# A conversion piece moved between angle and sine, and another order of the first weight loads, in a fused attention, mixture-of-experts and feed-forward kernel

## The chip, the cores and the metric

The kernel runs on one core of a Trainium2 chip. The metric is device microseconds for one execution; lower is better. The engines are TensorE (PE, its weight loads apart as PEld), VectorE (DVE), ScalarE (ACT), GpSimd (POOL) and SyncE (SP), which issues most of the DMAs.

## The reference, cut to what matters

Three stages follow one another. The change is in the third, and its weights are the only thing of it that earlier stages touch.

```python
# attention with a sigmoid: x = concat over heads of sigmoid(q k^T / 8 - log 448) v   -> [1792, 768]
# mixture of experts, top 1 of 8 by the gate, two matmuls with a relu, scaled           -> [1792, 768]
def _moe2_ref(x, w_in, w_out):          # x [1792, 768], w_in [768, 2048], w_out [2048, 768]
    h = x @ w_in
    g = h * np.cos(h)
    return (g @ w_out).astype(np.float32)
```

The inputs of the feed-forward weights arrive as float64, 512 of them per partition in a piece, and have to be turned into pairs of float32 numbers (high and low part) before TensorE can use them.

## The kernel before

**Conversion.** `w_in` and `w_out` are cut into 48 pieces, listed in `conv_list`: six of `w_in`, six of `w_out`, and so on. `conv_step(False)` does the following for the next piece: it finishes the piece before it (`conv_end`), stores that piece's two halves to DRAM (`conv_store`: `wi_d` or `wo_d` from `chi` and `clo`, 256 KB each, on SP's queue), loads the raw data of the piece after it (`conv_load`: `craw`, 512 KB, two buffers, SP's queue), and runs the first half of its own piece. The first half (L154 to L158) is an absolute value and a copy on ACT, a maximum on POOL, and two operations on DVE. The second half (L160 to L163) is four operations on DVE. It runs at the next `conv_end`, which stands in `product`, behind the product and ahead of the split into high and low parts; `load_w` calls `conv_end` too, where the weight to be loaded needs that piece. Of the 48 pieces, 23 are begun in the attention stage and 17 in the expert stage, so eight (40 to 47) are left for the feed-forward.

**Feed-forward.** The tokens are handled in four blocks of 3 or 4 times 128 tokens, and the 2048 inner columns in 16 chunks of 128. A unit u is one block and one chunk. For each unit there is:

- `load_w(u)`: the weights `wi` (768 KB) and `wo` (768 KB) of the chunk, on SP's queue, into rings of six buffers; it also stores what pieces are finished. `er` is the first buffer of the ring for `wi`; it is loaded for unit 0 in the expert stage already
- `up(u)`: 18 matmuls (L1109 to L1111) into a PSUM tile `ph`, from one pair of banks that the transposes below share
- `take(u)`: ACT copies `ph` to `p` (L1118)
- `angle(u)`: five operations on DVE (L1123 to L1127), from `p` to `r`
- `cosine(u)`: an absolute value and a sine on ACT (L1132, L1133), on `r`
- `product(u)`: `r` times `p` on DVE (L1138), then the second half of a piece if one is open, then the split: `gh` on ACT (L1142), `gl` on DVE (L1143)
- `down(u)`: 24 matmuls (L1169, L1170) with `gh`, `gl` and `wo`

All engines work in program order. The loop is pipelined: iteration u does `load_w(u + 5)`, `product(u + 1)`, `up`, `take` and `angle` of u + 2, `cosine(u + 2)` and `down(u)`. In iterations 8 to 13 of a block, `turn_y` also transposes 128 columns of the next block's tokens between `up(u + 2)` and `down(u)` (four transposes on PE, L1094, a copy on ACT, L1096, a subtraction on DVE, L1098). In iterations 1 to 4 a gather of the next block's tokens is issued on POOL's queue. Before the loop, `turn_first` transposes the first block, and units 0 to 2 are begun.

Of the kernel before, what the change touches and what calls it, by code (L numbers as in the profile page):

```python
# [54 lines left out]
def tile_attn_moe_cos(ctx: ExitStack, tc: tile.TileContext, q, k, v, wg, wog, w1, w2, w_in, w_out, out):  # L55
# [66 lines left out]
    conv_list = []  # L122
# [7 lines left out]
    def conv_load(i):  # L130
        if i >= len(conv_list):
            return
        which, h, r = conv_list[i]
        raw = craw[i % 2]
        if which == "i":
            src = w_in[r * P : (r + 1) * P, h * CW : (h + 1) * CW].bitcast(U32)
            nc.sync.dma_start(raw.rearrange("p f t -> p (f t)"), src)
        else:
            src = wo_in[h][:, :, r * CO : (r + 1) * CO].bitcast(U32)
            nc.sync.dma_start(raw.rearrange("p (two f) t -> p two (f t)", two=2), src)  # L140

    def conv(i):
        if i >= len(conv_list):
            return
        which, h, r = conv_list[i]
        raw = craw[i % 2]
        low, high = raw[:, :, 0], raw[:, :, 1]

        ta = cta
        tb = conv_p.tile([P, CW], U32, tag="ctb", name="ctb")  # L150
        tu = conv_p.tile([P, CW], F32, tag="ctu", name="ctu")
        hi = conv_p.tile([P, CW], U32, tag="chi", name="chi", bufs=2)
        lo = conv_p.tile([P, CW], F32R, tag="clo", name="clo", bufs=2)
        nc.scalar.activation(ta.bitcast(F32), high.bitcast(F32), AF.Abs)  # L154
        nc.gpsimd.tensor_scalar(ta.bitcast(F32), ta.bitcast(F32), LEAST, None, op0=ALU.max)  # L155
        nc.scalar.activation(tu, low, AF.Copy, scale=2.0**-52)
        nc.vector.tensor_scalar(tb, high, 0x1FF, None, op0=ALU.bitwise_and)
        nc.vector.scalar_tensor_tensor(tu, tb, 2.0**-20, tu, op0=ALU.mult, op1=ALU.add)  # L158
        yield
        nc.vector.tensor_scalar(ta, ta, 3, 0x3FFFF000, op0=ALU.logical_shift_left, op1=ALU.bitwise_and)  # L160
        nc.vector.scalar_tensor_tensor(hi, high, 0xC0000000, ta, op0=ALU.bitwise_and, op1=ALU.bitwise_or)  # L161
        nc.vector.tensor_scalar(tb, hi, 0xFF800000, None, op0=ALU.bitwise_and)
        nc.vector.tensor_tensor(lo, tu, tb.bitcast(F32), op=ALU.mult)  # L163
        conv_out.append((which, h, r, (hi.bitcast(F32), lo.bitcast(F32))))

    def conv_store():
        while conv_out:
            which, h, r, parts_ = conv_out.pop()
            for t, f in enumerate(parts_):
                if which == "i":  # L170
                    c0 = h * CW // P
                    nc.sync.dma_start(
                        wi_d[c0 : c0 + CW // P, :, t, r, :].rearrange("c p f -> p c f"),
                        f.rearrange("p (c f) -> p c f", f=P),
                    )
                else:
                    nc.sync.dma_start(
                        wo_to[h, t][:, :, r * CO : (r + 1) * CO], f.rearrange("p (two f) -> p two f", two=2)
                    )

    conv_at = [0]

    def conv_step(whole=True):
        conv_end()
        conv_store()
        conv_load(conv_at[0] + 1)
        conv_rest.append(conv(conv_at[0]))
        next(conv_rest[0], None)
        conv_at[0] += 1
        if whole:  # L190
            conv_end()
# [3 lines left out]
    def conv_end():  # L195
        while conv_rest:
            next(conv_rest.pop(), None)
# [444 lines left out]
    def load_w(u, which="io"):  # L642
        c = u % NFF
        ready = max(i for i, (which, h, _) in enumerate(conv_list) if h == (c * P // CW if which == "i" else c // 2))
        while conv_at[0] <= ready:
            conv_step()
        if conv_at[0] - 1 <= ready:
            conv_end()
        conv_store()
        if "i" in which:  # L650
            wi = ring_i[u % NRING]
            nc.sync.dma_start(wi.bitcast(F32), wi_d[c].rearrange("p t k f -> p (t k f)"))
            wi = wi.rearrange("p (t k f) -> p t k f", t=2, k=KD)
            parts["i", u] = (wi[:, 0], wi[:, 1])
        if "o" in which:
            wo = ring_o[u % NRING]
            nc.sync.dma_start(wo.bitcast(F32), wo_d[c * P : (c + 1) * P].rearrange("p t e -> p (t e)"))
            parts["o", u] = (wo[:, :DM], wo[:, DM:])
# [386 lines left out]
    with ExitStack() as st:  # L1045
# [12 lines left out]
        def take_ids(bi):  # L1058
            t0, nt = blocks[bi]
            for i in range(nt):  # L1060
                nc.vector.tensor_copy(tids[:, t0 + i : t0 + i + 1], ygt[i][:, DM : DM + 1].bitcast(I32))

        def turn_first():
            t0, nt = blocks[0]
            yh = yp.tile([P, KD, 512], F32R, tag="yh", name="yh")
            yl = yp.tile([P, KD, 512], F32R, tag="yl", name="yl")
            yts[0] = (yh, yl)
            spare = [ps_o.tile([P, 512], F32, tag=f"o{i}", name="pt") for i in range(3)]
            spare = [t[:, : 3 * P].rearrange("p (k t) -> p k t", t=P) for t in spare]
            for k0 in range(0, KD, 3):  # L1070
                for i in range(nt):
                    cols = slice(i * P, (i + 1) * P)
                    pt = spare[(i + nt * (k0 // 3)) % len(spare)]
                    for kc in range(3):
                        nc.tensor.transpose(
                            pt[:, kc, :], ygt[i][:, (k0 + kc) * P : (k0 + kc + 1) * P], ident
                        )
                    yhv, ylv = yh[:, k0 : k0 + 3, cols], yl[:, k0 : k0 + 3, cols]
                    nc.scalar.activation(yhv, pt, AF.Copy)
                    nc.vector.tensor_tensor(ylv, pt, yhv.bitcast(F32), op=ALU.subtract)  # L1080
            take_ids(0)
# [34 lines left out]
        def take(u, ph):  # L1116
            p = gpool.tile([P, 512], F32, tag="p", name="p", bufs=2)[:, : ph.shape[1]]
            nc.scalar.activation(p, ph, AF.Copy)  # L1118
            return p
# [10 lines left out]
        def cosine(u):  # L1130
            p, r = rs[u]
            nc.scalar.activation(r, r, AF.Abs)  # L1132
            nc.scalar.activation(r, r, AF.Sin, bias=b_half, scale=-1.0)  # L1133
# [15 lines left out]
        def down(u):  # L1149
# [14 lines left out]
            for i in range(nt):  # L1164
# [13 lines left out]
                if c == NFF - 1 and (own or i % 2 == 1):  # L1178
                    for j in (i,) if own else (i - 1, i):
# [3 lines left out]
                        done.append((t0 + j, osb))  # L1183
                    if u == N - 1:
                        put()

        def put():
            if done:
                i, osb = done.pop(0)

                at = yp.tile([P, 1], I32, tag="at", name="at", bufs=4)
                nc.gpsimd.tensor_copy(at, tids[:, i : i + 1])
                rows = nc.gpsimd.indirect_dma_start(  # L1193
                    out=out[:, :],
                    out_offset=bass.IndirectOffsetOnAxis(ap=at, axis=0),
                    in_=osb,
                    in_offset=None,
                )
                if i > 0:
                    tc.declare_no_dep(rows.ins, group="rows", reason="rows apart")  # L1200
                tc.add_to_no_dep_group("rows", rows.ins)

        N = len(units)
        conv_load(conv_at[0])
        load_w(0, "o")
        load_w(1)
        load_w(2)
        turn_first()
        load_w(3)
        p0 = take(0, up(0))  # L1210

        nc.scalar.activation(scs[:, 0:1], b_half, AF.Sin)
# [7 lines left out]
        cosine(1)  # L1220
        for u in range(N):
            bi, c = units[u]
            if u > 1 and conv_at[0] < len(conv_list):
                conv_step(False)
            if u + 5 < N:
                load_w(u + 5)
            turn = ()
            if bi + 1 < len(blocks):
                if 1 <= c < 5:
                    gather_y(bi + 1, c - 1)  # L1230
                if 8 <= c < 8 + KD:
                    turn = turn_y(bi + 1, c - 8)
            if u + 1 < N:
                product(u + 1)
            if u + 2 < N:
                angle(u + 2, take(u + 2, up(u + 2)) if u > 0 else p2)
            for _ in turn:
                pass
            if c < NFF - 1 and u + 2 < N:
                cosine(u + 2)  # L1240
            down(u)
            if c > 1:
                put()
            if c == NFF - 1 and u + 2 < N:
                cosine(u + 2)
# [28 lines left out]
```

## Time and profile before

| | |
|---|---|
| median of 3 runs | 1103.56 us (1101.51 to 1110.1) |
| the profiled execution: time, and span of its trace | 1106.36 us, 1104.6 us |
| TensorE clock granted, mean | 0.983 |
| PE busy | 1046.0 us (95%) |
| PEld busy | 835.7 us (76%) |
| DVE busy | 697.5 us (63%) |
| ACT busy | 484.7 us (44%) |
| POOL busy | 184.6 us (17%) |

Times in the trace count from the start of the span. The feed-forward begins at about 600 us and lasts to the end; its first block is the stretch from 600 to about 760 us. Matmuls overlap: each shows some 0.39 us, and they start 0.23 us apart. So a stall of PE is read from the starts.

### The profile page before, as it was taken

How to read it: one execution, taken by the hardware profiler on the slowest of the kernel's cores; microseconds unless marked ns; L12 is line 12 of the kernel's file. 1: busy time of each engine (PE TensorE's matmuls, PEld its weight loads, DVE VectorE, ACT ScalarE, POOL GpSimd, SP SyncE). 2: the span in 40 equal slices, each digit the busy share in tenths (PEclk: the TensorE clock that was granted, in tenths of full speed). 3: DMA queues.
4: the chain of work that ended last, by engine and by line, in shares of the span. 5: the costliest groups of instructions: out<-in, count | busy, mean ns of one | idle time of the engine just before them, and what ended most of it. 6: DMA issues, size and time to landing. Idle time of an engine off the chain costs nothing. (4 is left out here: it accounts for less than half of the span.)

```text
span 1104.6 us, 16903 instructions
## 1 busy us (share of the span) xinstructions
PE 1046.0 (95%) x5836; PEld 835.7 (76%) x5836; DVE 697.5 (63%) x1229; ACT 484.7 (44%) x706; POOL 184.6 (17%) x189
## 2 busy tenths in 40 slices
PE   7999998889999998998997999799999999999997
PEld 4555554468877886786786788688888899999996
DVE  3778778576667458658656577756545555565553
ACT  6777675432435246345344333343333343334332
POOL 4443332521110212211111021101100020001001
PEclk9999999989999999999899999999999999999999
DMA  7999896635488439939835988565755477667741
GB/s 192 267 290 304 248 270 178 213 105 196 138 292 293 137 99 350 323 126 361 264 116 176 414 292 295 189 260 195 255 207 190 171 261 301 255 248 279 253 176 43
DMA packets 118788, 254.68 MB, mean 231 GB/s; under 512 B 9440, under 2 KB 66016, under 8 KB 118688
## 3 DMA queue, kind: packets, MB, share of 16 engines
q1 hardware_dynamic: 114768, 234.19, 62.7%
q0 software_dynamic: 3920, 19.28, 4.8%
q8 instruction: 48, 0.79, 0.3%
q14 instruction: 52, 0.43, 0.1%
HBM read 207.02 MB, written 46.41 MB: 229 GB/s over the span
## 5 line engine op out<-in xcount | busy, mean ns | idle before, releaser
L1169 PE MATMUL o<-wo,gh 128*128 128x512 f32 x448 | 168.4, 397 | 0.0
L155 POOL TENSOR_SCALAR cta<-cta 128x512 f32<-128x512 f32 x48 | 75.8, 1578 | 473.2 <-ACT cta L154 449.0
L1109 PE MATMUL ph<-yh,wi 128*128 128x512 f32 (+1 forms) x318 | 116.2, 365 | 6.7 <-ACT p L1118 4.2
L1110 PE MATMUL ph<-yl,wi 128*128 128x512 f32 (+1 forms) x318 | 115.9, 365 | 0.0
L1111 PE MATMUL ph<-yh,wi 128*128 128x512 f32 (+1 forms) x318 | 115.7, 364 | 0.0
L1132 ACT ACTIVATE r<-r 128x512 f32<-128x512 f32 (+1 forms) x64 | 37.0, 578 | 175.2 <-DVE r L1127 173.5
L301 ACT ACTIVATE aT<-sc,b_sig 112x896 f32<-112x896 f32 x96 | 91.6, 1005 | 46.7 <-PE sc L298 45.4
L1170 PE MATMUL or<-wo,gh 128*128 128x256 f32 x384 | 108.3, 282 | 0.0
L1169 PEld LDWEIGHTS o<-wo,gh 128*128 128x128 f32 x448 | 84.2, 188 | 17.1
L242 PE MATMUL p<-w1h,xh 128*128 128x512 f32 x228 | 93.9, 412 | 0.5 <-ACT xh L234 0.5
L243 PE MATMUL p<-w1l,xh 128*128 128x512 f32 x228 | 91.2, 400 | 0.0
L244 PE MATMUL p<-w1h,xl 128*128 128x512 f32 x228 | 91.0, 399 | 0.0
L1169 PE MATMUL o<-wo,gl 128*128 128x512 f32 x224 | 88.4, 395 | 0.3 <-DVE gl L1143 0.3
L305 PE MATMUL av<-aT,v 112*64 112x448 f32 x384 | 84.5, 563 | 0.0
L1138 DVE TENSOR_TENSOR r<-r,p 128x512 f32<-128x512 f32 (+1 forms) x64 | 39.9, 624 | 65.8 <-ACT r L1133 65.8
L1193 POOL DMA_INDIRECT out_dram<-osb,at x14 | 14.2, 1016 | 364.2 <-DVE osb L1182 272.9
L1170 PEld LDWEIGHTS or<-wo,gh 128*128 128x128 f32 x384 | 72.3, 188 | 0.8
L1109 PEld LDWEIGHTS ph<-yh,wi 128*128 128x128 f32 x318 | 60.1, 189 | 15.7 <-ACT p L1118 4.5
L1118 ACT ACTIVATE p<-ph 128x512 f32<-128x512 f32 (+1 forms) x64 | 34.7, 541 | 75.0 <-PE ph L1111 75.0
L1123 DVE TENSOR_SCALAR t<-p 128x512 f32<-128x512 f32 (+1 forms) x64 | 25.1, 392 | 66.5 <-ACT p L1118 66.5
L709 ACT ACTIVATE hh<-pht 128x512 fp32r<-128x512 f32 x38 | 22.8, 599 | 100.2 <-PE pht L706 96.3
L1111 PEld LDWEIGHTS ph<-yh,wi 128*128 128x128 f32 x318 | 60.1, 189 | 6.5
(257 smaller groups left out, 2437.0 us busy)
## 6 DMA issues: line engine op xcount, KB each, us to landing
rw<-in_moe_w_dram SPq DMA_DIRECT2D x64, 768.0 KB, 6.7
wo<-wo_d SPq DMA_DIRECT2D x64, 768.0 KB, 4.5
wi<-wi_d SPq DMA_DIRECT2D x53, 768.0 KB, 6.0
craw<-in_moe_w_in_dram SPq DMA_DIRECT2D x25, 512.0 KB, 6.0
craw<-in_moe_w_out_dram SPq DMA_DIRECT2D x24, 512.0 KB, 5.3
er<-wi_d SPq DMA_DIRECT2D x11, 768.0 KB, 6.4
ys_d<-ysb SPq DMA_DIRECT2D x19, 384.5 KB, 3.5
wi_d<-chi SPq DMA_DIRECT2D x24, 256.0 KB, 3.7
```

What stands on the lines that cost most here:

```text
L155: nc.gpsimd.tensor_scalar(ta.bitcast(F32), ta.bitcast(F32), LEAST, None, op0=ALU.max)
L242: nc.tensor.matmul(ps, xh[:, kc], wh, start=first, stop=False)
L243: nc.tensor.matmul(ps, xh[:, kc], wl, start=False, stop=False)
L244: nc.tensor.matmul(ps, xl[:, kc], wh, start=False, stop=last)
L301: nc.scalar.activation(aT[:, c], ps[:, :, :S], AF.Sigmoid, bias=b_sig[:CP], scale=1.0 / math.sqrt(D))
L305: nc.tensor.matmul(pav[D * j : D * j + D, :S], t["v"][:, j, c, :], aT[:, c, j], start=c == 0, stop=c == NC - 1)
L1109: nc.tensor.matmul(ph[:, :w], wih[:, kc], yh[:, kc, :w], start=kc == 0, stop=False)
L1110: nc.tensor.matmul(ph[:, :w], wih[:, kc], yl[:, kc, :w], start=False, stop=False)
L1111: nc.tensor.matmul(ph[:, :w], wil[:, kc], yh[:, kc, :w], start=False, stop=kc == KD - 1)
L1138: nc.vector.tensor_tensor(r, r, p, op=ALU.mult)
L1169: nc.tensor.matmul(acc[i], g[:, ts_], w[:, :512], start=f, stop=l)
L1170: nc.tensor.matmul(acc["r", i], g[:, ts_], w[:, 512:], start=f and (own or i % 2 == 0), stop=l, skip_group_check=True,)
```

## The change

In the loop, the call that begins the next piece moves. It stood at the head of iteration u, from u = 2 on. Now it stands behind `angle(u + 2)` (and behind the transposes' subtraction) and ahead of `cosine(u + 2)`, from u = 1 on. Ahead of the loop the order of the loads becomes: `wi` of units 1 and 2, `wo` of units 0 and 1, then the raw data of piece 40, `wi` of 3, `wo` of 2 and 3. It was: raw data of piece 40, `wo` of 0, then `wi` and `wo` of 1, of 2, of 3. `conv_store` runs with the first `load_w` in both, so the stores of piece 39 stood behind the raw data and now stand first.

```diff
         N = len(units)
+        load_w(1, "i")
+        load_w(2, "i")
+        load_w(0, "o")
+        load_w(1, "o")
+        turn_first()
         conv_load(conv_at[0])
-        load_w(0, "o")
-        load_w(1)
-        load_w(2)
-        turn_first()
-        load_w(3)
+        load_w(3, "i")
+        load_w(2, "o")
+        load_w(3, "o")
         p0 = take(0, up(0))
...
         for u in range(N):
             bi, c = units[u]
-            if u > 1 and conv_at[0] < len(conv_list):
-                conv_step(False)
             if u + 5 < N:
                 load_w(u + 5)
...
                 angle(u + 2, take(u + 2, up(u + 2)) if u > 0 else p2)
             for _ in turn:
                 pass
+            if u > 0 and conv_at[0] < len(conv_list):
+                conv_step(False)
             if c < NFF - 1 and u + 2 < N:
                 cosine(u + 2)
             down(u)
```

## Rows read from the trace of the kernel before

**Rows 1.** Waits of PE, 598 to 722 us: total, times, longest.

```profile
PE ph L1109 <- ACT p L1118: 5.9, 2, 4.2
PE pt L1075 <- DVE yl L1080: 2.6, 1, 2.6
PE ph L1109 <- DMA wi<-wi_d: 2.5, 2, 1.9
```

**Rows 2.** Timeline of PE, units 0 to 2: start, duration, [idle before, releaser].

```profile
613.16 0.39 PE L1111 MATMUL ph<-yh,er 128*128 128x512 f32 x1
614.17 0.50 PE L1109 MATMUL ph<-yh,wi 128*128 128x512 f32 x1 [0.62 <-DMA wi<-wi_d]
...
620.46 0.50 PE L1109 MATMUL ph<-yh,wi 128*128 128x512 f32 x1 [1.87 <-DMA wi<-wi_d]
...
624.68 0.40 PE L1169 MATMUL o<-wo,gh 128*128 128x512 f32 x1
```

**Rows 3.** Timeline of PE, iterations 8 to 10.

```profile
692.29 0.48 PE L1169 MATMUL o<-wo,gh 128*128 128x512 f32 x1
...
713.89 0.50 PE L1109 MATMUL ph<-yh,er 128*128 128x512 f32 x1 [1.70 <-ACT p L1118]
...
718.55 0.47 PE L1169 MATMUL o<-wo,gh 128*128 128x512 f32 x1
```

**Rows 4.** Chain that ended last: the transposes of iterations 10 and 11.

```profile
718.36 0.44 PE pyt L1094 x4
727.09 0.44 PE pyt L1094 x4
```

**Rows 5.** Timeline of DVE, one unit with a conversion piece.

```profile
664.37 0.42 DVE L1123 TENSOR_SCALAR t<-p 128x512 f32<-128x512 f32 x1
...
670.00 0.69 DVE L158 SCALAR_TENSOR_TENSOR ctu<-ctb,ctu 128x512 f32<-128x512 uint32 x1 [2.22 <-ACT ctu L156]
670.61 0.69 DVE L1138 TENSOR_TENSOR r<-r,p 128x512 f32<-128x512 f32 x1
...
674.06 0.42 DVE L1123 TENSOR_SCALAR t<-p 128x512 f32<-128x512 f32 x1
```

**Rows 6.** Timeline of ACT, the same unit: the piece's first operation.

```profile
668.76 0.65 ACT L154 ACTIVATE cta<-craw 128x512 f32<-128x512 f32 x1
```

**Rows 7.** Timeline of DVE, units 1 to 3, without a piece.

```profile
620.84 0.42 DVE L1123 TENSOR_SCALAR t<-p 128x512 f32<-128x512 f32 x1
...
628.79 0.42 DVE L1123 TENSOR_SCALAR t<-p 128x512 f32<-128x512 f32 x1
...
633.31 0.69 DVE L1138 TENSOR_TENSOR r<-r,p 128x512 f32<-128x512 f32 x1 [1.46 <-ACT r L1133]
...
635.31 0.42 DVE L1123 TENSOR_SCALAR t<-p 128x512 f32<-128x512 f32 x1
```

**Rows 8.** Timeline of DVE, iterations 8 and 9, the last piece.

```profile
703.11 0.42 DVE L1123 TENSOR_SCALAR t<-p 128x512 f32<-128x512 f32 x1
...
708.75 0.69 DVE L158 SCALAR_TENSOR_TENSOR ctu<-ctb,ctu 128x512 f32<-128x512 uint32 x1 [1.40 <-ACT ctu L156]
...
712.01 0.68 DVE L1138 TENSOR_TENSOR r<-r,p 128x512 f32<-128x512 f32 x1
```

**Rows 9.** Timeline of SP, the first DMAs of the feed-forward.

```profile
604.47 0.34 SPq L137 DMA_DIRECT2D craw<-in_moe_w_in_dram  x1
...
606.65 1.04 SPq L652 DMA_DIRECT2D wi<-wi_d  x1
```

**Rows 10.** Timeline of POOL, then of DVE, in the attention stage.

```profile
101.14 1.49 POOL L155 TENSOR_SCALAR cta<-cta 128x512 f32<-128x512 f32 x1 [4.97 <-ACT cta L154]
...
101.20 0.84 DVE L157 TENSOR_SCALAR ctb<-craw 128x512 uint32<-128x512 uint32 x1
```

**Rows 11.** Windows: length, busy time by engine, granted clock, DMA share, GB/s.

```profile
640.00:680.00 40.00, 40.00 (x204) 33.91 (x203) 29.20 (x53) 15.23 (x26) 9.91 (x8) 1.00 0.86 290
```

**Rows 12.** Instructions of the tile craw: times to landing of its 49 loads.

```profile
DMA to landing us min/median/max: 3.7/5.9/10.7
```

## The prediction

> **What bounds the kernel now.** I read the waits of PE first, because PE is 95% busy: only where it waits can a reordering win. In the stretch from 598 to 722 us PE waits 2.5 us for `wi` of units 1 and 2, and 5.9 us for the copy `p` [rows 1]. The 2.6 us for `yl` beside them belong to `turn_first`, whose operations keep their order; they stay. The same view from 722 us to the end lists no wait of PE at all, so nothing after the first block can be won, and what the first block saves is shortened from the whole.
>
> The timeline of PE then says what these waits cost with their consequences. At the start, `up(1)` begins at 614.17 though the last matmul of `up(0)` began at 613.16, `up(2)` at 620.46 after an idle 1.87, and `down(0)` at 624.68 [rows 2]. From `down(0)` to `down(8)` PE runs 67.61 us for eight units, 8.45 each, with almost no stall [rows 2, 3]. Then it takes 26.26 us from `down(8)` to `down(10)` [rows 3]; an undisturbed unit with transposes takes 8.73 (727.09 less 718.36) [rows 4].
>
> The timeline of DVE shows why. A unit with a piece lasts 9.69 us there (664.37 to 674.06) [rows 5], a unit without one 6.52 (628.79 to 635.31) [rows 7]. PE needs 8.45. So the pieces make DVE and ACT the slower side for a while: they eat their lead, 1.24 us a unit, and by iteration 8 PE is caught. Within the 9.69, DVE idles 2.22 us ahead of L158 [rows 5]. ACT has the piece's two operations queued behind the sine, so L154 starts only at 668.76 [rows 6], and the product, queued on DVE behind L158, waits for them.
>
> **The change part by part.**
>
> Loads. Ahead of `wi` of unit 1 stood 512 KB of raw data, 512 KB of stores and 768 KB of `wo`; now only the stores stand there. SP starts at 604.47 as before, since nothing ahead of it changes. `wi` of unit 1 was issued at 606.65 and awaited until 614.17, a flight of at most 7.5 us [rows 2, 9]. Now two issues stand ahead of it instead of four, so it goes out at about 605.5. Even with the old flight it lands at 613.0, ahead of 613.4 (613.16 plus one start of 0.23), when `up(0)` is through. `wi` of unit 2 follows directly, 768 KB later; it is wanted 4.2 us after that. `wo` of unit 0 loses its place: ahead of it and with it are now 2.75 MB, where 2.5 MB had landed by 614.17 before, so it comes near 615 to 617. It is wanted at 621.8. If that cover of 5 us were gone, `down(0)` would wait by the excess.
> Sum for the start: `up(1)` at 613.4, two times 4.22 (624.68 less 620.46) [rows 2], so `down(0)` at 621.84 instead of 624.68: **2.84 us**. `gl(0)` is no hindrance: the DVE operation behind it starts at 620.84 [rows 7].
>
> The piece. Every operation of it stays; only its places in the queues change. On ACT its two operations now stand behind `take(u + 2)` and run while DVE does the angle. On DVE its first two operations stand behind the angle and run while ACT does absolute value and sine. The four of the second half keep their place behind the next product. On POOL the maximum stands behind the gather of the same iteration instead of ahead of it; it is wanted some 5 us later. On SP the two stores and the raw load now stand behind `load_w(u + 5)`, whose `wo` waits for `down(u - 1)`. That is over before the product that the stores wait for, so this costs nothing; were it late, the raw load would be late by as much (the slower rival below). Pieces start with iteration 1 instead of 2, and every weight finds as many of them done as before.
> New period of DVE with a piece: from angle to product 4.52 (628.79 to 633.31) [rows 7]. In it DVE waited 1.46 for the sine, and the piece's L157 and L158 (0.42 and 0.69) fit into that. From product to the next angle with four operations of a piece between, 3.45 (670.61 to 674.06) [rows 5]. Together **7.97 us** instead of 9.69, under PE's 8.45.
>
> Does that clear iterations 8 to 10? `take(2)` no longer holds back the absolute value of unit 1, so `angle(2)` starts at 620.84 + 4.52 + 2.00 = 627.36 (2.00 is product to angle without a piece, 633.31 to 635.31) [rows 7]. `angle(3)` follows at 633.88, and `angle(10)`, seven periods with a piece later, at 689.67, where it was 703.11 [rows 8]. The last piece is finished by `load_w(14)` ahead of the product; from angle to product that took 8.90 with a 1.40 wait for ACT [rows 8], so 7.50 now: product at 697.2. PE starts `up(12)` 1.88 after that product (712.01 to 713.89) [rows 3, 8], so it may at 699.1. PE itself gets there at 692.29 - 2.84 + 17.46 - 4.66 = 702.25 (4.66 is `up(12)` to `down(10)`) [rows 3, 4]. The margin is 3.2 us: no wait is left.
> Sum for the middle: 26.26 less two times 8.73 = **8.80 us**.
>
> One cost no row shows in this place: POOL's maximum will now run while DVE does `gl` and the angle. In the attention stage L157, issued 0.06 after POOL's L155, lasted 0.84 [rows 10], where its like lasts 0.42; it ended 0.90 after POOL's start, so DVE was held until 0.48 after that start. Bounds: nothing (a gain is excluded, since sharing speeds up neither) to 0.48 per piece. The eight pieces up to `up(12)` give at most 3.84 us, against the margin of 3.2: a wait of up to 0.6. I take none, since half the price already fits.
> [...]
>
> Sum: 2.84 + 8.80 = 11.64 us. Against the profiled execution (1106.36, span 1104.6) that gives 1094.7; that execution was 2.8 above the median of the runs. Against the median it gives 1103.56 - 11.64 = **1091.9 us**, 1.05% less.
>
> **The rivals.**
>
> *DVE stays the slower side.* If each piece costs DVE the 1.49 of POOL's operation [rows 10], the eight push `up(12)` to 699.1 + 11.9 = 711.0, 8.7 behind PE. That leaves 2.9 of the gain: **1100.7 us**. [...] Against it: the held time of 0.48 above. [...]
>
> *The loads come late all the same.* The stores, now first, might hold back `wi`, or `wo` of unit 0 might. Then the start's 2.84 go and the middle stays: **1094.7 us**. Against it are the flights above; for it, that the flight is taken from a queue with other neighbours.
>
> *Slower: the raw data arrive late.* ACT's absolute value and sine of a unit now stand behind the piece's two operations, and these wait for `craw`. It is issued when the piece before its predecessor is through, at about the start of an angle. If landing takes L, then four passes of ACT at 0.65 [rows 6] and 3.45 of DVE follow, over two units: twice the period is L + 6.05. It binds over PE's 8.45 from L = 10.85, and the change loses from the point where the eight pieces lose 3.2 + 11.64, that is 1.85 each, a period of 9.82, L = 13.6. At L = 15 the period is 10.5, and the time 1103.56 + (8 x 2.55 - 3.2 - 11.64) = **1109 us**. For it: DMA is busy 0.86 at a period of 9.69 [rows 11], which is 0.99 at 8.45. Against it: the 49 raw loads took 3.7 to 10.7 us [rows 12], and the weights that share the queue have three units of lead.
>
> **How the numbers follow.** The forecast gets 0.66, with 1089.5 to 1094 of its own: 2 us below the median is where the fastest run of before lay, and 0.6 is the open wait. The late loads get 0.14, the blocked DVE 0.14, the late raw data 0.06. The range 1088 to 1098 holds the first two cases with the runs' scatter and leaves out the other two. Faster by over 1% means below 1092.5; the forecast lies just beyond it, so a bit more than half of it counts there. 1% is about what a measurement of this kernel can tell from no change. Faster 0.45, within 1% 0.52, slower 0.03 (half of the last rival).
>
> **What the profile after would show.** PE without a wait for `wi` near 613 and 618, and `down(0)` some 3 us earlier. On DVE a period near 8.0 to 8.5 with no 2 us hole ahead of L158. No wait of PE for `p` in iterations 8 to 10, and the granted clock at 1.00 there. `wo` landing before 621. DVE operations beside POOL's maximum at 0.4 and 0.7, or up to 0.5 longer. The prediction is wrong if PE waits for `p` or `gl` in those iterations again, if ACT's L154 shows a wait for `craw`, or if the saved time turns up as a wait of PE in a later block, where I count none.

## The result, and the profile after

The changed kernel takes 1094.46 us (median of 13 runs, 1089.47 to 1101.38); before, 13 runs now, 1103.97 us. The ratio is 0.9913, 95% interval 0.9896 to 0.993: 9.6 us less, with an interval of 7.7 to 11.5. The profiled execution took 1094.78 us, with a span of 1093.0.

Three starts on PE cut the changed stretch into stages: the last matmul of the expert stage, `down(0)`, `down(8)` and `down(10)`. Every number in this table is the difference of two starts in the timeline of PE.

| kernel | to down(0) | down(0) to (8) | down(8) to (10) |
|---|---|---|---|
| before | 25.66 | 67.61 | 26.26 |
| the change | 22.06 | 67.05 | 19.65 |

That is 3.60, 0.56 and 6.61 us less, 10.77 together; another 0.84 lies ahead of the stretch, which the change does not touch. From `down(10)` to the last matmul both kernels take the same 377.7 us, so nothing is given back later.

The waits of PE of the changed kernel, 598 to 722 us, answer to [rows 1]:

```profile
PE pt L1075 <- DVE yl L1080: 2.5, 1, 2.5
PE pt L1075 <- DVEq L1018: 1.8, 1, 1.8
PE pyt L1094 <- DVE yl L1098: 1.3, 1, 1.3
PE ph L1109 <- ACT p L1118: 0.3, 1, 0.3
PE ph L1109 <- DMA wi<-wi_d: 0.2, 1, 0.2
```

The 5.9 for `p` are down to 0.3, the 2.5 for `wi` to 0.2. The 1.3 for `yl` of L1098 are new. The timeline of PE shows both places, and answers to [rows 2, 3]:

```profile
607.27 0.47 PE L1109 MATMUL ph<-yh,er 128*128 128x512 f32 x1
...
611.33 0.40 PE L1111 MATMUL ph<-yh,er 128*128 128x512 f32 x1
611.94 0.50 PE L1109 MATMUL ph<-yh,wi 128*128 128x512 f32 x1 [0.22 <-DMA wi<-wi_d]
...
620.24 0.40 PE L1169 MATMUL o<-wo,gh 128*128 128x512 f32 x1
...
687.29 0.48 PE L1169 MATMUL o<-wo,gh 128*128 128x512 f32 x1
...
697.15 0.33 PE L1094 MATMUL pyt<-ident,yg_r 128*128 128x128 f32 x1 [1.30 <-DVE yl L1098]
...
702.28 0.50 PE L1109 MATMUL ph<-yh,er 128*128 128x512 f32 x1 [0.27 <-ACT p L1118]
...
706.94 0.48 PE L1169 MATMUL o<-wo,gh 128*128 128x512 f32 x1
```

`up(1)` starts 0.61 after the last matmul of `up(0)`, where it was 1.01, and `up(2)` no longer waits. Between `down(8)` and `down(10)` two waits are left, of 1.30 and 0.27.

Not all of what the last stage lost before was waiting. Behind the longest wait, of 4.2 us, the matmuls were slower for a while before: those from 702.68 to 705.67 start 0.42 to 0.43 apart, those from 705.99 on 0.22 to 0.24. From the first to the last matmul of `up(11)` it took 5.60 us before and takes 3.88 after. The granted clock is 1.00 throughout this stage after; before, it was 0.83 in the window around `up(11)`:

```profile
700.00:710.00 10.00, 8.45 (x35) 6.94 (x36) 8.05 (x19) 4.08 (x7) 1.66 (x3) 0.83 0.21 78
```

DVE, one unit with a piece, answers to [rows 5], and the operations of ACT and POOL beside it to [rows 6]:

```profile
640.75 0.69 DVE L1123 TENSOR_SCALAR t<-p 128x512 f32<-128x512 f32 x1
641.48 0.43 DVE L1124 TENSOR_SCALAR t<-t 128x512 f32<-128x512 f32 x1
...
644.52 0.69 DVE L158 SCALAR_TENSOR_TENSOR ctu<-ctb,ctu 128x512 f32<-128x512 uint32 x1
645.54 0.69 DVE L1138 TENSOR_TENSOR r<-r,p 128x512 f32<-128x512 f32 x1 [0.32 <-ACT r L1133]
...
647.79 0.69 DVE L163 TENSOR_TENSOR clo<-ctu,ctb 128x512 fp32r<-128x512 f32 x1
648.40 1.10 DVE L1143 TENSOR_TENSOR gl<-r,gh 128x512 fp32r<-128x512 f32 x1
649.42 0.69 DVE L1123 TENSOR_SCALAR t<-p 128x512 f32<-128x512 f32 x1
```

```profile
646.80 0.58 ACT L1118 ACTIVATE p<-ph 128x512 f32<-128x512 f32 x1
647.33 0.68 ACT L154 ACTIVATE cta<-craw 128x512 f32<-128x512 f32 x1
```

```profile
648.09 1.74 POOL L155 TENSOR_SCALAR cta<-cta 128x512 f32<-128x512 f32 x1 [5.73 <-ACT cta L154]
```

The hole of 2.22 us ahead of L158 is gone, as forecast. L154 follows `p` at once. The period is 8.67 (640.75 to 649.42), though, and not 7.97. Two operations are longer than in any unit without a piece: `gl` with 1.10 instead of 0.69, and L1123 with 0.69 instead of 0.42. Both lie beside POOL's maximum, which runs from 648.09 to 649.83. 0.41 and 0.27 make 0.68 of the 0.70 that the period is too long. Six of the eight pieces look like this one; in the first, L1125 is held by 0.29, and in the last, L1123 and L1124 by 0.41 each.

### The profile page after: what moved, and what is told of

Same layout as the page of the kernel before. It is cut to its first block, busy times and chain, and to the rows that moved or that the text cites. A ratio compares the mean times of both kernels' runs of the same rounds, so it can differ in the third digit from the quotient of the medians.

```text
span 1093.0 us, 16911 instructions
## 1 busy us (share of the span) xinstructions
PE 1040.6 (95%) x5836; PEld 832.6 (76%) x5836; DVE 703.8 (64%) x1229; ACT 486.1 (44%) x706; POOL 186.1 (17%) x189
## 5 line engine op out<-in xcount | busy, mean ns | idle before, releaser
L1123 DVE TENSOR_SCALAR t<-p 128x512 f32<-128x512 f32 (+1 forms) x64 | 27.2, 425 | 65.7 <-ACT p L1118 65.7
L1109 PEld LDWEIGHTS ph<-yh,wi 128*128 128x128 f32 x318 | 59.7, 188 | 8.4 <-DMA wi<-wi_d 0.7
L1143 DVE TENSOR_TENSOR gl<-r,gh 128x512 fp32r<-128x512 f32 (+1 forms) x64 | 42.5, 664 | 36.4 <-ACT gh L1142 36.4
```

Source lines behind the costliest of these rows:

```text
L1109: nc.tensor.matmul(ph[:, :w], wih[:, kc], yh[:, kc, :w], start=kc == 0, stop=False)
L1143: nc.vector.tensor_tensor(gl[:, :w], r, gh[:, :w].bitcast(F32), op=ALU.subtract)
```

## The experiments

The question they had to settle was why the last stage gained 6.61 us where 8.80 were forecast. My theory was that GpSimd's maximum holds VectorE, at more places than I had priced. The rival was that the new order makes VectorE's own chain longer, whoever runs beside it. Two runs take the parts singly, four change what GpSimd does, one takes the pieces out.

**Loads alone** (e1_loads): the new order of the loads, with the pieces at the head of the iteration.

```diff
+            if u > 1 and conv_at[0] < len(conv_list):
+                conv_step(False)
             if u + 5 < N:
                 load_w(u + 5)
...
-            if u > 0 and conv_at[0] < len(conv_list):
-                conv_step(False)
```

> The new order of the first loads alone; the pieces stay at the head of the iteration. Theory (the middle is bound by VectorE, so PE's earlier start is mostly given back there): from the last matmul of the expert stage to down(0) some 2.8 to 3.6 us less than the 25.66 of before, but from down(8) to down(10) about 1.4 us more than 26.26, because VectorE's loop starts only 1.43 earlier while PE starts 2.84 earlier. Total gain about 1.4 us, ratio to before 0.9987. Rival (the parts add up): 26.26 stays, gain 2.8 us or more, ratio 0.9974.

Measured: 1101.77 us, ratio 0.9978 (0.9964 to 0.9992). Stages: 22.06, 69.28, 26.26. The waits of PE, 595 to 722 us:

```profile
PE ph L1109 <- ACT p L1118: 4.9, 2, 4.2
...
PE o L1169 <- DVE gl L1143: 1.7, 3, 1.1
```

The start gains its 3.60, and 1.67 of it is lost again. The amount is that of the theory (1.4), the place is not: PE catches up with VectorE two units earlier and waits for `gl` ahead of `down(8)`, and the last stage stays as it was. So the loads alone are worth some 2 us; the timed 2.4 would by itself also allow the rival's 2.8.

**The piece alone** (e2_piece): the old order of the loads, the piece between angle and sine.

```diff
-        load_w(1, "i")
-        load_w(2, "i")
+        conv_load(conv_at[0])
         load_w(0, "o")
-        load_w(1, "o")
+        load_w(1)
+        load_w(2)
         turn_first()
-        conv_load(conv_at[0])
-        load_w(3, "i")
-        load_w(2, "o")
-        load_w(3, "o")
+        load_w(3)
```

> The piece between angle and sine alone, with the old order of the loads. Theory (VectorE's loop decides, and PE comes 1.4 us later relative to it than with both parts): period of a unit with a piece 8.67 as with both, and the waits of PE in iterations 8 to 10, 1.57 us with both, shrink to about 0.2; from down(8) to down(10) about 18.2 us. Gain about 8 us, ratio 0.9927. Rival (the parts add up): 19.65 us from down(8) to down(10) as with both, gain 6.7 us, ratio 0.994.

Measured: 1095.05 us, ratio 0.9919 (0.99 to 0.9939). Stages: 25.37, 67.05, 18.44. The waits of PE, 595 to 722 us:

```profile
PE ph L1109 <- DMA wi<-wi_d: 2.7, 2, 1.9
...
PE ph L1109 <- ACT p L1118: 0.3, 1, 0.3
```

With PE later at the start, VectorE keeps more of its lead, and the 1.30 for the transposes are gone: 18.44 was expected as 18.2 by the theory and 19.65 by the rival. So the piece carries most of the gain. Stage by stage the two parts do not add, because an earlier start of PE is worth less where VectorE has little lead; but that is so with the piece moved and without it, and the sums agree: 1.93 us for the loads and 8.67 for the piece make 10.60 over the three stages, and the change gives 10.77.

**The maximum on VectorE** (e3_max_on_dve), in the eight pieces of the feed-forward:

```diff
-        nc.gpsimd.tensor_scalar(ta.bitcast(F32), ta.bitcast(F32), LEAST, None, op0=ALU.max)
+        eng = nc.vector if i >= CONV_EARLY else nc.gpsimd
+        eng.tensor_scalar(ta.bitcast(F32), ta.bitcast(F32), LEAST, None, op0=ALU.max)
```

> The change, with the maximum of the eight pieces of the feed-forward on VectorE in place of GpSimd, at the same place in the program. Theory (GpSimd's maximum holds VectorE twice a piece, 0.41 us at gl and 0.27 at the angle's first operation): one more operation of 0.46 on VectorE, of which 0.32 fit into its wait for the sine, but 0.70 less held; period 8.1 instead of 8.67, gl at 0.69 and L1123 at 0.42 in every unit, no wait of PE in iterations 8 to 10, 17.5 us from down(8) to down(10), and a time about 2 us under that of the change, ratio to before 0.990. Rival (the 0.70 comes from VectorE's own work in the new order, not from GpSimd): period 8.8 to 9.1, waits of PE grow by 1 to 3 us, ratio 0.992 to 0.994.

Measured: 1092.46 us, ratio 0.9903 (0.9883 to 0.9924). Stages: 21.73, 67.41, 17.62, and no wait of PE in iterations 8 to 10. DVE (the lines of the file are one higher from L156 on; L156 is the maximum):

```profile
644.19 0.42 DVE L1124 TENSOR_SCALAR t<-p 128x512 f32<-128x512 f32 x1
...
647.17 0.42 DVE L156 TENSOR_SCALAR cta<-cta 128x512 f32<-128x512 f32 x1
...
651.57 0.68 DVE L1144 TENSOR_TENSOR gl<-r,gh 128x512 fp32r<-128x512 f32 x1
652.17 0.42 DVE L1124 TENSOR_SCALAR t<-p 128x512 f32<-128x512 f32 x1
```

VectorE has one operation more and a period of 7.98, shorter by 0.69. `gl` and the angle's first operation are back at 0.68 and 0.42. The rival, by which the period would grow, falls.

**No maximum** (e4_no_max):

```diff
-        nc.gpsimd.tensor_scalar(ta.bitcast(F32), ta.bitcast(F32), LEAST, None, op0=ALU.max)
+        if i < CONV_EARLY:
+            nc.gpsimd.tensor_scalar(ta.bitcast(F32), ta.bitcast(F32), LEAST, None, op0=ALU.max)
```

> The change without the maximum of the eight pieces of the feed-forward; this leaves out the clamp of very small weights. Theory (contention with GpSimd is the whole of the 0.70): period 7.97 as predicted, no wait of PE in iterations 8 to 10, 17.5 us from down(8) to down(10), time equal to that with the maximum on VectorE, ratio 0.990. Rival (GpSimd has no part in it): period 8.67, gl still 1.10 long, PE's waits of 1.57 us stay, ratio 0.9913 as with the change.

Measured: 1091.01 us, ratio 0.9891 (0.9869 to 0.9912). Stages: 21.33, 67.05, 17.65, no wait of PE in iterations 8 to 10. DVE:

```profile
645.64 0.42 DVE L1124 TENSOR_SCALAR t<-p 128x512 f32<-128x512 f32 x1
...
653.02 0.68 DVE L1144 TENSOR_TENSOR gl<-r,gh 128x512 fp32r<-128x512 f32 x1
653.62 0.42 DVE L1124 TENSOR_SCALAR t<-p 128x512 f32<-128x512 f32 x1
```

A period of 7.98, where the prediction had 7.97. Without GpSimd beside it the chain is what the rows of before gave.

**The maximum twice** (e6_double_max):

```diff
         nc.gpsimd.tensor_scalar(ta.bitcast(F32), ta.bitcast(F32), LEAST, None, op0=ALU.max)
+        if i >= CONV_EARLY:
+            nc.gpsimd.tensor_scalar(ta.bitcast(F32), ta.bitcast(F32), LEAST, None, op0=ALU.max)
```

> The change, with GpSimd's maximum done twice in each of the eight pieces of the feed-forward. [...] Rival (the 0.70 has another cause): period 8.67, waits 1.57.

Measured in one run: 1093.71 us; stages 23.26, 67.05, 22.42. DVE, and then POOL:

```profile
645.66 1.10 DVE L1145 TENSOR_TENSOR gl<-r,gh 128x512 fp32r<-128x512 f32 x1
646.68 0.69 DVE L1125 TENSOR_SCALAR t<-p 128x512 f32<-128x512 f32 x1
647.41 0.71 DVE L1126 TENSOR_SCALAR t<-t 128x512 f32<-128x512 f32 x1
```

```profile
645.34 1.75 POOL L155 TENSOR_SCALAR cta<-cta 128x512 f32<-128x512 f32 x1 [4.43 <-ACT cta L154]
647.17 1.54 POOL L157 TENSOR_SCALAR cta<-cta 128x512 f32<-128x512 f32 x1
```

The second maximum holds the angle's second operation (0.71 instead of 0.43), and the period is 8.98, which is 0.31 above that of the change. PE's waits in iterations 8 to 10 grow from 1.57 to 4.1 us. The whole time is lower than that of the change all the same, because the stages ahead took 5.0 us less in this execution (the last matmul of the expert stage at 593.16 instead of 598.18).

**A fill in place of the maximum** (e7_pool_write): GpSimd writes the tile and reads nothing.

```diff
-        nc.gpsimd.tensor_scalar(ta.bitcast(F32), ta.bitcast(F32), LEAST, None, op0=ALU.max)
+        if i < CONV_EARLY:
+            nc.gpsimd.tensor_scalar(ta.bitcast(F32), ta.bitcast(F32), LEAST, None, op0=ALU.max)
+        else:
+            nc.gpsimd.memset(ta.bitcast(F32), 1.0)
```

> The change, with a fill by GpSimd in place of its maximum in the eight pieces of the feed-forward: the same tile is written, none is read; the high parts of these weights become a constant. [...]

Measured in one run: 1089.81 us; stages 21.37, 67.05, 17.57. POOL, then DVE, in the first piece, in a middle one and in the last:

```profile
630.14 0.53 POOL L158 MEMSET cta<- 128x512 f32 x1 [22.19 <-ACT cta L154]
...
645.10 0.53 POOL L158 MEMSET cta<- 128x512 f32 x1 [6.05 <-ACT cta L154]
...
685.98 0.53 POOL L158 MEMSET cta<- 128x512 f32 x1 [8.27 <-ACT cta L154]
```

```profile
630.12 0.82 DVE L1127 TENSOR_SCALAR t<-t 128x512 f32<-128x512 f32 x1
...
645.42 0.68 DVE L1146 TENSOR_TENSOR gl<-r,gh 128x512 fp32r<-128x512 f32 x1
646.03 0.42 DVE L1126 TENSOR_SCALAR t<-p 128x512 f32<-128x512 f32 x1
...
685.95 0.84 DVE L1126 TENSOR_SCALAR t<-p 128x512 f32<-128x512 f32 x1
```

`gl` (L1146) starts 0.32 into the fill, which has 0.21 left, and is not held at all; in the change it started 0.31 into the maximum and was held by 0.41. The fill reads nothing, but it is also shorter than the maximum, 0.53 against 1.74, so which of the two spares `gl` is not taken apart. Where an operation of the angle starts 0.02 or 0.03 ahead of the fill, in the first piece and in the last, it lasts 0.82 and 0.84 instead of 0.43 and 0.42. The period is 8.37 in the first piece and 7.98 in the middle ones, where the fill is over before L1126 starts.

**All pieces ahead of the feed-forward** (e5_pieces_early):

```diff
-CONV_EARLY = 40
+CONV_EARLY = 48
...
                 if s == 0:
                     split2(2)
                     split2(3)
+                elif 2 <= s < 10:
+                    conv_step()
```

> The change, with all 48 pieces done before the feed-forward: expert slots 2 to 9 do a second piece in their middle. Theory (once no piece is left in the feed-forward, nothing but PE bounds its first block, and the expert stage has room on VectorE beside PE): no wait of PE in iterations 8 to 10, 17.5 us from down(8) to down(10), expert stage as long as before, time that of the kernel with the maximum on VectorE, some 1092 us. Rival (the expert stage has no room: PE already waits there 14.2 us in 11 slots for hr from VectorE): each extra piece, about 3.4 us of VectorE, delays hr by 1 to 3 us, 8 to 24 us in all, 1100 to 1115 us.

Measured: 1120.42 us, ratio 1.0135 (1.0104 to 1.0165). Stages of the feed-forward: 22.75, 67.04, 17.58. The waits of PE in the expert stage, 260 to 627 us:

```profile
PE pht L706 <- DVE hr L700: 22.5, 9, 5.0
PE pht L706 <- DVEq L754: 8.9, 4, 4.4
PE py L719 <- DVE hl L710: 2.8, 4, 0.9
PE py L719 <- DVEq L733: 2.0, 3, 0.9
```

The feed-forward is as short as without pieces, but the last matmul of the expert stage comes at 626.88 instead of 598.18. These waits sum to 36.2 us, 16 more than the 20.1 of the same view of the change; the rest of the 28.7 was not traced. The rival holds, and more than that: its 1100 to 1115 us were too low. The expert stage has no room for a second piece in these slots, and the gap between angle and sine is the better place for the last pieces.

## Why the prediction was right, and where it was not

- **The time.** 1094.46 lies in the range, but 0.5 above the 1089.5 to 1094 that the forecast had for its own. It is almost the time of the rival by which the loads come late, 1094.7; that is chance, since `wi` made a wait of only 0.22. By stage, the start gained 0.76 more than forecast, the stage behind it 0.56 where nothing was forecast, and the last one 2.19 less: 10.77 in the traces instead of 11.64. The timed 9.6 lies lower by another 1.2, which its interval covers.
- **The signs.** The hole ahead of L158 is gone and the granted clock is 1.00 in the last stage, as forecast. Two signs failed. The period is 8.67, above the 8.0 to 8.5 that were named, and PE waits for `p` again, 0.27 in iteration 10, which was to mean that the prediction is wrong. The direction and the two mechanisms held, the claim that no wait is left did not.
- **The loads**, 2.84 forecast. From the start of `up(0)` to `down(0)` it took 16.54 before [rows 2] and 12.97 after. Of the 3.57, 0.96 is `up(0)` itself, beside which the granted clock was 0.69 in this execution and 0.50 before (below); this part is luck. The other 2.61 lie behind it, and most of them are the waits, 2.49 before and 0.22 after. `wi` of unit 1 was issued at 604.70 and flew 7.2 us, so the bound taken from the old flight was good; the margin of 0.4 was eaten by the faster `up(0)`, hence the wait of 0.22. `wo` of unit 0 made no wait.
- **The stage from `down(0)` to `down(8)`.** The 8.45 that the prediction reads as PE's undisturbed unit is a mean of 8.32 for most units and 9.23 for the last. So 0.56 was to be won there.
- **VectorE's chain**, 7.97 forecast from [rows 5, 7]. Right, 7.98 with GpSimd out of the way.
- **GpSimd beside VectorE** is the step that failed: the bounds, "nothing" to "0.48 per piece", and the "I take none". It measured 0.70. The row of before [rows 10] had shown one meeting; here the maximum meets two operations, first `gl` (0.41), then the angle's first (0.27). The trace of before had more to say. Two maxima on POOL, each with an operation of DVE beside it:

```profile
173.33 1.49 POOL L155 TENSOR_SCALAR cta<-cta 128x512 f32<-128x512 f32 x1 [7.20 <-ACT cta L154]
174.52 0.58 DVE L157 TENSOR_SCALAR ctb<-craw 128x512 uint32<-128x512 uint32 x1
...
640.42 1.49 POOL L155 TENSOR_SCALAR cta<-cta 128x512 f32<-128x512 f32 x1 [29.06 <-ACT cta L154]
640.92 0.69 DVE L158 SCALAR_TENSOR_TENSOR ctu<-ctb,ctu 128x512 f32<-128x512 uint32 x1 [2.22 <-ACT ctu L156]
```

  In [rows 10], L157, which lasts 0.42 when alone, began 0.06 after the maximum and was held until 0.48 after its start. At 174.52 it began 1.19 after the maximum and was held until 1.35. L158, with two inputs, began 0.50 after the maximum and was not held. So it is not the overlap alone that counts, but where in the maximum an operation begins: the holds end at 0.48 and at 1.35. The other 22 operations of pieces that are held beside a maximum in the trace of before bear this out: their holds end at 0.46 to 0.48, counted without what the maximum lasts over 1.49. The change shows the same two ends, 0.25 later, as its maximum is 0.25 longer (1.74): `gl` begins 0.31 after the start of the maximum and is held until 0.72, L1123 begins 1.33 after it and is held until 1.60. Both holds could have been priced from the trace of before.
- **The margin of 3.2 us** fell with that price. Eight pieces at 0.70 are 5.6 us, and less 3.2 that is a loss of 2.4; measured were 2.0 (17.62 and 17.65 without GpSimd's part, 19.65 with it, 17.46 forecast). Where the loss shows was not foreseen. The transposes of iteration 9 need the bank that `yl` of iteration 8 frees, and they waited 1.30, `up(12)` only 0.27. Their own margin, 3.4 in e4_no_max, was no smaller than that of `up(12)`, so it was the price that failed and not the choice of the operation. By these 2 us the forecast lay beyond 1% and the measured time within it, though the intervals do not part the change from the kernels without GpSimd's part (0.9903 and 0.9891).
- **Rivals.** Of "DVE stays the slower side" the hold was real and the size half of it: its 1.49 per piece is an estimate from the length of POOL's operation [rows 10], which no run shows; measured were 0.70, with holds that end at 0.48 and 1.35 of 1.49 (POOL's spans are rough in this profile). The raw loads never held ACT back. The first in the loop took 13.3 us to land, the longest of the 49, but it was issued at 625.01 and wanted at 638.66, so it came 0.3 us before its time. The busy share of DMA rose from 0.86 to 0.92 in the window of [rows 11], less than the 0.99 worked out. The landing times of `craw` and this window, after:

```profile
DMA to landing us min/median/max: 3.9/6.0/13.3
```

```profile
640.00:680.00 40.00, 40.00 (x202) 33.81 (x201) 37.00 (x60) 16.76 (x27) 10.19 (x7) 1.00 0.92 330
```

## What to carry to other kernels

A side job in an engine's queue costs what the main chain waits behind it, not its own duration (here the same operations made a period of 9.69 us before and 8.67 after): put its slow part where the main chain has handed over to another engine, and look for the hole in both queues. Price GpSimd beside VectorE by where in the GpSimd operation each VectorE operation begins, since here one maximum held two of VectorE's, by 0.41 and 0.27. Moving 0.42 us of work onto the busier engine made that engine faster here by 0.69 a unit, and the kernel with it is the fastest of those that leave nothing out (0.9903, though its interval does not part it from the change's 0.9913). Where a margin decides, give the costs that eat it a price from every row that shows them, not from one; and check every operation that waits for the slower side, since the wait can turn up at another one than last time.

## What the runs showed that was not expected

The first matmuls of the feed-forward run at a lower granted clock for a time that differs from trace to trace: before, the second to the fifth of `up(0)` start 0.42 to 0.43 apart and those from the seventh on 0.22 to 0.24, in the change 0.23 to 0.24 from the second on. The window is the 5 us that begin 6 us after the last matmul of the expert stage. In the change, PE was busy for 1.6 of the 6 us ahead of it and is busy throughout in it:

```profile
604.18:609.18 5.00, 5.00 (x23) 4.25 (x24) 3.71 (x11) 2.46 (x5) 0.00 (x0) 0.69 0.91 288
```

The granted clock was 0.50 before, 0.55 in e1_loads and e2_piece, 0.66 in e3_max_on_dve, 0.69 in the change, and 0.70 in e4_no_max. The program of e1_loads is that of the change up to there, with 0.55 against 0.69, so the edits do not explain it. This moves `down(0)` by up to 1 us. What sets it is open.

GpSimd's maximum differs in length, too: it takes 1.74 in six pieces of the change, where L163 was under way as it started, and 1.49 in the feed-forward before, where VectorE was idle as it started. The attention stage of before has both lengths too, 1.74 for the maximum at 24.09, with L163 under way from 23.79.
